# Row clamps and first splits reordered, and float32 operands for one more attention tile, in a fused attention, gated MLP and routed expert kernel

## The chip, the cores and the metric

The kernel runs on one core of a Trainium2 chip. The metric is the device time of one execution in microseconds: the median of three runs. One further execution was recorded by the profiler; durations below come from that one. The engines are TensorE (PE, with PEld for its weight loads), VectorE (DVE), ScalarE (ACT), GpSimd (POOL) and SyncE (SP), which issues most DMAs.

## The reference

What is computed, with the shapes of this case:

```python
# attention: q, k, v (2, 8, 768, 64); n_global 8, n_local 96
scores = q @ k.T / 8 - slope[h] * dist      # local window of 96, and 8 global columns; the rest masked
a = softmax(scores)                          # + 1e-9 in the denominator
x = (a @ v) as (1536, 512)
# gated MLP, d_ff 1536
xn = x / rms(x) * rms_g
x = (silu(xn @ w_gate) * (xn @ w_val)) @ w_out
# routed experts: 8 experts, d_ff 1024, two per token
noisy = x @ w_router + log1p(exp(x @ w_noise)) * noise
top2 = the two largest of noisy; weights = softmax over the two
out[t] = sum over the two experts e of weight * (relu(x[t] @ w1[e]) @ w2[e])
```

The MLP's three weights arrive as 64-bit floats and are brought to float32 in the kernel, from pairs of 32-bit words.

## The kernel before, in words

Everything stays in one program on one core, and the order of each engine's instructions is made by a planner at build time, which plays the program through in its own simulated time and takes the instructions in the order in which they become ready there, earlier lines of the program first. `follow(a, b)` (L262) adds an edge with no wait in it: the planner puts `a` behind `b` in the order. On the chip each engine works through its queue strictly in that order, so an instruction that waits holds up all that is queued behind it.

**Attention.** The 1536 tokens are 12 tiles of 128, six per batch (`NB`). Tile `ti` attends to its own and the preceding tile's keys, and to the first 32 columns. A tile is worked through in four steps of two heads (`scores`, `turn` and `values`, at L358, L388 and L416). Matmuls with full precision are made in two ways. Tiles below `F32T` (L133, value 5: tiles 0 to 4) use float32 operands, one float32 product for the scores and one for the values, which the profile shows as two records each. Tiles from `F32T` on split each operand into a high and a low part: three float32r products for the scores (L372 to L374), and for the values five products of 16-bit parts (L445 to L447). The splits are made on ACT and DVE (L325 to L331, L407, L408) and on POOL (`vsplit`, L300). Tile 5 is the first tile with split operands and the last of batch 0, so `prep` (L306) has a branch (L341 to L350) that splits the keys which it takes over from tile 4, and `values` (L429) splits tile 4's values anew. Tile 6 starts batch 1 and takes nothing over.

**MLP.** `VISITS` lists blocks of two or four tiles by chunks of the 12 slices of d_ff. One step of a block runs `up` for gate and value (matmuls into `pg`, `pv` or one `pz`, L613), `hidden` (L616 and on: `u` on ACT and DVE, `dh` on ACT at L625, `dl`), and `down` (matmuls into `acc`, L639), one step behind. The rest of attention is strewn among the first blocks by `side`. A tile's normalised rows are turned by `norm` (L514): transposes into `px` (L518), `xTh` on ACT (L523), `xTl` on DVE (L524).

**Weights of the MLP.** `conv` (L544) loads one block of words (L553), takes Abs on ACT (L558), clamps (L559, on POOL for later blocks), shifts and combines on DVE (L561, L565, L566), and splits (L568, L569). After attention a pool "b" opens in its place; some of the first blocks loaded then have their words in that pool (`spare`, L547).

**Experts.** `route` scores and ranks tokens for a group of tiles and scatters token number and weight to a table in DRAM by indirect DMAs on POOL (L779). There are units of gathered rows: units 0 and 1 for the first 256 and the remaining rows of the expert that leads early, and units 2 to 8 for the other experts. Unit 0 starts under the last MLP blocks, before the last tiles are routed. For each unit `slots` fetches its table rows (`me`, L820, on SP), clamps the row numbers to the table's end (`ic`, L829, on DVE); `gather` (L838) fetches 128 rows by an indirect DMA on POOL; `turn` transposes them on TensorE (L848) and splits them into `gh` on ACT and `gl` on DVE (L850, L851). `run` (L860 and on) goes through 8 slices: `split` (L592) copies an expert's slab on ACT (L597) and subtracts on POOL or DVE (L599); `up` (L874) gives `zh` and `zl` (L878, L879); `down` (L890 or L896) adds up; the rows are scattered into the output (L932), for later units on top of what stands there (`old`, L856). A slab's load is issued by L804 and L807, the next unit's turns and loads run inside the unit before.

Of the kernel before, what the change touches and what calls it, by code (L numbers as in the profile page):

```python
# [9 lines left out]
F32 = mybir.dt.float32  # L10
# [9 lines left out]
P = 128  # L20
# [85 lines left out]
def fused(ctx: ExitStack, tc: tile.TileContext, q, k, v, n_global, n_local, w_gate, w_val, w_out,  # L106
# [23 lines left out]
    LAG = 8  # L130
    NRAW = {"a": 12, "b": 7}
    NACC = 8
    F32T = 5  # L133
    N2 = 4
    slopes = [2.0 ** (-8.0 * (h + 1) / H) for h in range(H)]

# [125 lines left out]
    def follow(a, b):  # L262
        tc.add_manual_dep(a, b.name, mybir.DependencyInfo(mybir.DependencyClass.NoSync, mybir.DependencyReason.DATA),
                          reason="order")
# [41 lines left out]
    def prep(ti, wide):  # L306
        b, i = divmod(ti, NB)
        t0 = i * P
        nblk = 1 if i == 0 else 2
        W = nblk * P  # L310
        C0 = 2 * P - W
        qn, kn = state.pop(("in", ti))
        full = ti < F32T
        if full:
            kT = [at.tile([P, NP, 2 * P], F32, name=f"kT{ti}", tag="kT0", bufs=2)] * 2
            qT = [at.tile([P, NP, P], F32, name=f"qT{ti}", tag="qT0", bufs=2)] * 2
        else:
            kT = [at.tile([P, NP, 2 * P], F32R, name=f"kT{ti}_{x}", tag=f"kT{x}", bufs=2) for x in range(2)]
            qT = [at.tile([P, NP, P], F32R, name=f"qT{ti}_{x}", tag=f"qT{x}", bufs=2) for x in range(2)]
        for src, dh, dl, sc in ((kn, kT[0][:, :, P:], kT[1][:, :, P:], 1.0), (qn, qT[0], qT[1], -(D ** -0.5))):  # L320
            pt = bank("t", wide, f"pt{ti}")
            p3 = pt.rearrange("p (a b) -> p a b", a=NP)
            for c in range(NP):
                nc.tensor.transpose(p3[:, c, :], src.rearrange("p (a t) d -> p a (t d)", a=NP)[:, c, :], ident)
            nc.scalar.activation(dh, p3, AF.Copy, scale=sc)  # L325
            if full:
                continue
            if sc == 1.0:
                nc.vector.tensor_sub(dl, p3, dh.bitcast(F32))
            else:  # L330
                nc.vector.scalar_tensor_tensor(dl, p3, sc, dh.bitcast(F32), op0=ALU.mult, op1=ALU.subtract)  # L331

        def same(dst, src):
            nc.gpsimd.tensor_scalar(dst, src if src.dtype == F32 else src.bitcast(F32), 1.0, 0.0, op0=ALU.mult, op1=ALU.add)
        parts = 1 if full else 2
        if i == 0:
            kg = [at.tile([P, NP, 32], F32 if full else F32R, name=f"kg{ti}_{x}", tag=f"kg{x}", bufs=1) for x in range(parts)]
            for x in range(parts):
                same(kg[x], kT[x][:, :, P:P + 32])
            state["kg"] = kg  # L340
        elif ti == F32T:  # L341
            ok, pk = state["kg"][0], state["kT"][0][:, :, P + 32:]
            kg = [at.tile([P, NP, 32], F32R, name=f"kg{ti}_{x}", tag=f"kh{x}", bufs=1) for x in range(2)]
            same(kg[0], ok)
            nc.gpsimd.tensor_sub(kg[1], ok, kg[0].bitcast(F32))
            same(kT[0][:, :, 32:P], pk)
            nc.gpsimd.tensor_sub(kT[1][:, :, 32:P], pk, kT[0][:, :, 32:P].bitcast(F32))
            for x in range(2):
                same(kT[x][:, :, :32], kg[x])
            state["kg"] = kg  # L350
        else:
            for x in range(parts):
                same(kT[x][:, :, :32], state["kg"][x])
                same(kT[x][:, :, 32:P], state["kT"][x][:, :, P + 32:])
        state["kT"] = kT
        state["cur", ti] = (W, C0, nblk, kT, qT)
# [59 lines left out]
    def values(u, wide):  # L416
        ti, pr = divmod(u, NP)
        nblk = state["cur", ti][2]
        if pr == 0:
            i = ti % NB  # L420
            if i > 1:
                grows(ti)
            own = [state["own", ti]]
            if i:
                own.insert(0, state["own", ti - 1])
            if ti < F32T:
                state["vs", ti] = [a[0].rearrange("p h d -> p (h d)") for a in own]
            else:
                if ti == F32T:  # L429
                    own[0] = state["own", ti - 1] = vsplit(ti - 1, own[0][0])  # L430
                state["vs", ti] = [(halves(a)[1], halves(b)[1], halves(a)[0]) for a, b in own]
        vs = state["vs", ti]
        ph, pl = state.pop(("pt", u))
        if pr == 0:
            state["po", ti] = bank("o", wide, f"po{ti}")
        po = state["po", ti]
        for t in range(2):
            h = pair[pr][t]
            hs = slice(h * D, (h + 1) * D)
            n = 0  # L440
            if ti < F32T:
                for j in range(nblk):
                    nc.tensor.matmul(po[:, hs], (ph, pl)[t][:, j, :], vs[j][:, hs], start=(j == 0), stop=(j == nblk - 1))
                continue
            for j in range(nblk):  # L445
                for lhs, x in ((ph, 0), (ph, 1), (ph, 2), (pl, 0), (pl, 1)):
                    nc.tensor.matmul(po[:, hs], lhs[:, t, j, :], vs[j][x][:, hs], start=(n == 0),  # L447
                                     stop=(n == 5 * nblk - 1))
                    n += 1
        if pr == NP - 1:  # L450
            rs = sb.tile([P, H], F32, name=f"rs{ti}", tag="rs", bufs=2)
            nc.vector.tensor_scalar(rs, state.pop(("sm", ti)), PSC, PSC * 1e-9, op0=ALU.mult, op1=ALU.add)
            nc.vector.reciprocal(rs, rs)
            x = sb.tile([P, DM], F32, name=f"x{ti}", tag="n2", bufs=N2)
            nc.vector.tensor_mul(x.rearrange("p (h d) -> p h d", h=H), po.rearrange("p (h d) -> p h d", h=H),
                                 rs.rearrange("p (h o) -> p h o", o=1).broadcast_to([P, H, D]))
            state["x", ti] = rms(ti, x)
            del state["cur", ti]
# [55 lines left out]
    def norm(ti, x, wide):  # L514
        pt = bank("t", wide, f"px{ti}")
        p3 = pt.rearrange("p (a b) -> p a b", a=DC)
        for c in range(DC):
            nc.tensor.transpose(p3[:, c, :], x[:, c * P:(c + 1) * P], ident)  # L518
        g, tt = divmod(ti, ST)
        if tt == 0:  # L520
            xTh[g] = sb.tile([P, ST, DC, P], F32R, name=f"xTh{g}", tag="xTh", bufs=3)
            xTl[g] = sb.tile([P, ST, DC, P], F32R, name=f"xTl{g}", tag="xTl", bufs=3)
        nc.scalar.activation(xTh[g][:, tt], p3, AF.Copy)  # L523
        nc.vector.tensor_sub(xTl[g][:, tt], p3, xTh[g][:, tt].bitcast(F32))  # L524


    pools = {"a": sb}
# [16 lines left out]
    def conv(nm, f, src):  # L544
# [14 lines left out]
        (nc.gpsimd if late else nc.vector).tensor_scalar(w, w, HIGH, LOW, op0=ALU.min, op1=ALU.max)  # L559
        wi = w.bitcast(I32)  # L560
        sh = nc.vector.tensor_scalar(wi, wi, 3, 0x3FFFFFF8, op0=ALU.logical_shift_left, op1=ALU.bitwise_and)  # L561
        if f:
            after(ab, "A", min(f, 3) - 1)
            after(sh, "V", min(f, 3) - 1)
# [27 lines left out]
    def split(key, u):  # L592
        pid = "ab" + key[1:]
        src = raw[pid][:, "ab".index(key[0])]
        f = int(key.split("_")[1])
        wp = pools["b"].tile([P, 2, 512], F32R, name=f"s{key}_{u}", tag="ws", bufs=3)
        nc.scalar.activation(wp[:, 0], src, AF.Copy)  # L597
        pool = u == 0 and f < 5 if key[0] == "b" else u >= 2 and f < 3
        (nc.gpsimd if pool else nc.vector).tensor_sub(wp[:, 1], src, wp[:, 0].bitcast(F32))  # L599
        return wp[:, 0], wp[:, 1]  # L600

    x2t = {}

    accs = {}

    def up(f, nm, t0, nt, pz):
# [9 lines left out]
    def hidden(ci, f, t0, nt, pg, pv):  # L616
        GN = nt * P
        hp = pools["b"] if nt > 2 else sb
        u = hp.tile([P, GN], F32, name=f"u{t0}_{f}", tag="u", bufs=1)
        nc.scalar.activation(u, pg, AF.Tanh, scale=0.5)  # L620
        nc.vector.scalar_tensor_tensor(u, u, 1.0, pg, op0=ALU.add, op1=ALU.mult)
        nc.vector.scalar_tensor_tensor(u, u, 0.5, pv, op0=ALU.mult, op1=ALU.mult)
        dh = hp.tile([P, GN], F32R, name=f"dh{t0}_{f}", tag="dh", bufs=2)
        dl = hp.tile([P, GN], F32R, name=f"dl{t0}_{f}", tag="dl", bufs=2)
        nc.scalar.activation(dh, u, AF.Copy)  # L625
        (nc.gpsimd if ci < len(CHUNKS) - 1 else nc.vector).tensor_sub(dl, u, dh.bitcast(F32))  # L626
        return dh, dl

# [180 lines left out]
    class Unit:  # L809
# [13 lines left out]
        def slots(self):  # L823
# [2 lines left out]
                self.fetch()  # L826
            me = self.me
            ic = sb.tile([P, NS], I32, name=f"ic{n}", tag="ic", bufs=3)
            nc.vector.tensor_scalar(ic[:, :ns], me[:, :ns, 0], self.rows - 1, None, op0=ALU.min)  # L829
            self.ic = ic  # L830
            self.gh = sb.tile([P, DC, CAP], F32R, name=f"gh{n}", tag="xTh", bufs=3)
            self.gl = sb.tile([P, DC, CAP], F32R, name=f"gl{n}", tag="xTl", bufs=3)
# [300 lines left out]
```

## Time and profile before

| | us |
|---|---|
| median of three runs | 823.5 (823.29 to 825.07) |
| the profiled execution | 823.71 |
| its span, first to last instruction | 821.9 |
| TensorE busy | 785.8, 96% of the span |
| VectorE, ScalarE, GpSimd busy | 464.1, 358.2, 302.3 |
| mean granted clock of TensorE | 0.990 of full speed |

A row of the profile names the engine, the line, the operation, the tile written and the tiles read, and the count of merged instructions (x4); a bracket at its end gives how long the engine had stood idle just before, and what ended that wait. A float32 matmul shows as two records. Matmuls are pipelined: a record's duration holds the pipeline's length, so the price of a group is the time from its start to the start of the next. "PEclk" is the TensorE clock that was granted in a stretch, as a share of full speed.

### The profile page before, as it was taken

The numbers are of one execution on the slowest core, as the hardware profiler recorded it, in microseconds if no ns is written. First come the engines' busy times: TensorE is split into PE (matmuls) and PEld (weight loads), VectorE is DVE, ScalarE is ACT, GpSimd is POOL, SyncE is SP. The second block draws the span as 40 slices with busy tenths as digits, with TensorE's granted clock in tenths as the row PEclk, the third lists the DMA queues.
The fourth block names the chain that finished last, engine by engine and source line by source line (L and its number), as shares of the span: only waits on it lengthen the run. The fifth ranks groups of instructions, "written<-read, shape, count | busy, mean of one in ns | idle before, by whom it ended". The sixth has DMA issues, their size and how long they took to land. (4 is left out here: it accounts for less than half of the span.)

```text
span 821.9 us, 13918 instructions
## 1 busy us (share of the span) xinstructions
PE 785.8 (96%) x5092; PEld 695.1 (85%) x5097; DVE 464.1 (56%) x1075; ACT 358.2 (44%) x803; POOL 302.3 (37%) x343
## 2 busy tenths in 40 slices
PE   6999999999989999999999997999999999999993
PEld 3678899898978888889998985888999999999982
DVE  4876756666578888424535466544444445445551
ACT  4666656565455344113332463533333434343430
POOL 6354334232068565100423045351424343434311
PEclk9999999999999999999999999999999999999997
DMA  9544313151043330001115303983373729272010
GB/s 198 153 127 117 104 32 73 39 155 53 2 146 112 104 126 26 1 1 52 27 27 137 121 27 98 324 272 120 100 212 121 236 92 279 80 244 74 35 38 34
DMA packets 116808, 88.78 MB, mean 108 GB/s; under 512 B 49417, under 2 KB 100617, under 8 KB 116736
## 3 DMA queue, kind: packets, MB, share of 16 engines
q1 hardware_dynamic: 105136, 65.09, 28.4%
q0 software_dynamic: 7120, 19.27, 7.0%
q10 hardware_dynamic: 4480, 3.49, 1.7%
q8 instruction: 42, 0.69, 0.4%
q14 instruction: 30, 0.25, 0.1%
HBM read 75.18 MB, written 13.34 MB: 108 GB/s over the span
## 5 line engine op out<-in xcount | busy, mean ns | idle before, releaser
L874 PE MATMUL pz<-gh,sa 128*128 128x256 f32 (+7 forms) x576 | 158.1, 340 | 1.8 <-DVE sa L599 0.8
L874 PEld LDWEIGHTS pz<-gh,sa 128*128 128x128 f32 x576 | 104.0, 190 | 8.0 <-DVE sa L599 1.3
L874 PE MATMUL pz<-gl,sa 128*128 128x256 f32 (+7 forms) x288 | 97.6, 339 | 0.9 <-DVE gl L851 0.9
L639 PE MATMUL acc<-wo,dh 128*128 128x512 f32 x288 | 89.7, 404 | 3.6 <-ACT dh L625 3.6
L890 PE MATMUL ac<-zh,sb 128*128 128x480 f32 (+4 forms) x320 | 86.3, 364 | 0.0
L878 ACT ACTIVATE zh<-pz 128x256 fp32r<-128x256 f32 (+7 forms) x72 | 35.1, 487 | 109.9 <-PE pz L874 109.3
L879 DVE SCALAR_TENSOR_TENSOR zl<-pz,zh 128x256 fp32r<-128x256 f32 (+7 forms) x72 | 39.7, 552 | 67.1 <-ACT zh L878 66.9
L597 ACT ACTIVATE sa<-wab 128x512 fp32r<-128x512 f32 x72 | 45.3, 630 | 68.8 <-PE ac L890 40.5
L613 PE MATMUL pz<-xTh,wv 128*128 128x256 f32 x352 | 73.8, 286 | 0.0
L613 PE MATMUL pz<-xTh,wg 128*128 128x256 f32 x352 | 72.6, 285 | 1.0 <-ACT xTh L523 0.7
L639 PEld LDWEIGHTS acc<-wo,dh 128*128 128x128 f32 x288 | 51.2, 189 | 13.9 <-ACT dh L625 4.6
L838 POOL DMA_INDIRECT xg<-x2d,ic x30 | 30.2, 1006 | 88.4 <-PE pg L848 48.3
L613 PEld LDWEIGHTS pz<-xTh,wg 128*128 128x128 f32 x352 | 58.3, 190 | 4.6 <-ACT xTh L523 0.9
L599 DVE TENSOR_TENSOR sa<-wab,sa 128x512 fp32r<-128x512 f32 x51 | 35.3, 693 | 45.4 <-ACT sa L597 45.3
L890 PEld LDWEIGHTS ac<-zh,sb 128*128 128x128 f32 x320 | 57.9, 188 | 3.2
L779 POOL DMA_INDIRECT metad<-meta,si x24 | 24.8, 1033 | 96.4 <-DVE si L758 90.3
L613 PEld LDWEIGHTS pz<-xTh,wv 128*128 128x128 f32 x352 | 57.6, 189 | 0.8 <-issue 0.3
L626 POOL TENSOR_TENSOR dl<-u,dh 128x256 fp32r<-128x256 f32 (+1 forms) x38 | 36.4, 957 | 58.6 <-ACT dh L625 41.0
L383 ACT ACTIVATE p<-s,mx 128x256 f32<-128x256 f32 (+1 forms) x96 | 46.2, 483 | 26.8 <-DVE mx L380 26.8
L874 PEld LDWEIGHTS pz<-gl,sa 128*128 128x128 f32 x288 | 54.6, 190 | 3.8 <-DVE gl L851 1.1
L639 PE MATMUL acc<-wo,dl 128*128 128x512 f32 x144 | 53.4, 401 | 0.0
L599 DVE TENSOR_TENSOR sb<-wab,sb 128x512 fp32r<-128x512 f32 x67 | 48.1, 719 | 8.9 <-ACT sb L597 8.0
(257 smaller groups left out, 1888.9 us busy)
## 6 DMA issues: line engine op xcount, KB each, us to landing
wab<-in_moe_w_dram SPq DMA_DIRECT2D x128, 256.0 KB, 4.9
rg<-in_moe_w_gate_dram SPq DMA_DIRECT2D x12, 512.0 KB, 3.7
rv<-in_moe_w_val_dram SPq DMA_DIRECT2D x12, 512.0 KB, 3.6
ro<-in_moe_w_out_dram SPq DMA_DIRECT2D x12, 512.0 KB, 3.5
kn<-in_k_dram SPq DMA_DIRECT2D x12, 256.0 KB, 3.5
qn<-in_q_dram SPq DMA_DIRECT2D x12, 256.0 KB, 4.1
vn<-in_v_dram SPq DMA_DIRECT2D x12, 256.0 KB, 5.3
out_dram<-zero SPq DMA_DIRECT2D x1, 3072.0 KB, 14.0
```

The source lines that it names most:

```text
L383: nc.scalar.activation(p[:, :W], s[:, :W], AF.Exp, scale=-1.0, bias=mx[:, h:h + 1], accum_out=sm[:, h:h + 1])
L597: nc.scalar.activation(wp[:, 0], src, AF.Copy)
L599: (nc.gpsimd if pool else nc.vector).tensor_sub(wp[:, 1], src, wp[:, 0].bitcast(F32))
L613: nc.tensor.matmul(pz, a[:, cs], x[:, tt:tt + nt, c, :], start=(n == 0), stop=(n == 3 * DC - 1))
L626: (nc.gpsimd if ci < len(CHUNKS) - 1 else nc.vector).tensor_sub(dl, u, dh.bitcast(F32))
L639: nc.tensor.matmul(acc[t], a[:, tt], w, start=(f == CHUNKS[ci][0] and n == 0), stop=(end and n == 2))
L779: st = nc.gpsimd.indirect_dma_start(out=metad, out_offset=bass.IndirectOffsetOnAxis(ap=si[:, t, kk:kk + 1], axis=0), in_=meta[:, G0[g] + t ...
L838: self.last = nc.gpsimd.indirect_dma_start(out=xg[:m], out_offset=None, in_=x2d[:self.rows], in_offset=bass.IndirectOffsetOnAxis(ap=self.i ...
L874: nc.tensor.matmul(pz[:, :cap], a[:, cs], x[:, c, :cap], start=(k == 0), stop=(k == 3 * DC - 1))
L878: nc.scalar.activation(dh[:, :cap], pz[:, :cap], AF.Relu)
L879: nc.vector.scalar_tensor_tensor(dl[:, :cap], pz[:, :cap], 0.0, dh[:, :cap].bitcast(F32), op0=ALU.max, op1=ALU.subtract)
L890: nc.tensor.matmul(acc[c][:, :cap], w[:, c * P:(c + 1) * P], a[:, :cap], start=(f == 0 and k == 0), stop=(f == FB2 - 1 and k == 2))
```

## The change

There are four edits. `F32T` becomes `NB`, 6, so that tile 5 too works with float32 operands; the branches that joined tile 4 to tile 5 go. In `conv`, the Abs and the first shift of the first three blocks with words in pool "b" follow the `xTh` and `xTl` of the tile normalised last. In `split`, the ACT copies of unit 0's slices 0 and 1 follow the fourth-last `dh` of the MLP (`marks[-4]`). The clamp `ic` of all nine units moves from DVE to POOL.

```diff
@@ -130,7 +130,7 @@
-    F32T = 5
+    F32T = NB
@@ -337,16 +337,6 @@
-        elif ti == F32T:
-            ok, pk = state["kg"][0], state["kT"][0][:, :, P + 32:]
-            kg = [at.tile([P, NP, 32], F32R, name=f"kg{ti}_{x}", tag=f"kh{x}", bufs=1) for x in range(2)]
-            same(kg[0], ok)
-            nc.gpsimd.tensor_sub(kg[1], ok, kg[0].bitcast(F32))
-            same(kT[0][:, :, 32:P], pk)
-            nc.gpsimd.tensor_sub(kT[1][:, :, 32:P], pk, kT[0][:, :, 32:P].bitcast(F32))
-            for x in range(2):
-                same(kT[x][:, :, :32], kg[x])
-            state["kg"] = kg
@@ -426,8 +416,6 @@
             else:
-                if ti == F32T:
-                    own[0] = state["own", ti - 1] = vsplit(ti - 1, own[0][0])
                 state["vs", ti] = [(halves(a)[1], halves(b)[1], halves(a)[0]) for a, b in own]
@@ -520,8 +508,9 @@
-        nc.scalar.activation(xTh[g][:, tt], p3, AF.Copy)
-        nc.vector.tensor_sub(xTl[g][:, tt], p3, xTh[g][:, tt].bitcast(F32))
+        hi = nc.scalar.activation(xTh[g][:, tt], p3, AF.Copy)
+        lo = nc.vector.tensor_sub(xTl[g][:, tt], p3, xTh[g][:, tt].bitcast(F32))
+        state["normed"] = hi.ins, lo.ins
@@ -559,6 +548,9 @@
         sh = nc.vector.tensor_scalar(wi, wi, 3, 0x3FFFFFF8, op0=ALU.logical_shift_left, op1=ALU.bitwise_and)
+        if spare and turns["words"] < 6:
+            follow(ab.ins, state["normed"][0])
+            follow(sh.ins, state["normed"][1])
@@ -594,13 +586,15 @@
-        nc.scalar.activation(wp[:, 0], src, AF.Copy)
+        cp = nc.scalar.activation(wp[:, 0], src, AF.Copy)
+        if u == 0 and f < 2:
+            follow(cp.ins, marks[-4])
@@ -622,7 +616,7 @@
-        nc.scalar.activation(dh, u, AF.Copy)
+        marks.append(nc.scalar.activation(dh, u, AF.Copy).ins)
@@ -826,7 +820,7 @@
-            nc.vector.tensor_scalar(ic[:, :ns], me[:, :ns, 0], self.rows - 1, None, op0=ALU.min)
+            nc.gpsimd.tensor_scalar(ic[:, :ns], me[:, :ns, 0], self.rows - 1, None, op0=ALU.min)
```

## Rows read from the trace of the kernel before

**Rows 1.** The page, part 1: busy us, share, instructions.

```profile
PE 785.8 (96%) x5092; PEld 695.1 (85%) x5097; DVE 464.1 (56%) x1075; ACT 358.2 (44%) x803; POOL 302.3 (37%) x343
```

**Rows 2.** Stretches: us; PE, PEld, DVE, ACT, POOL busy (x instructions); PEclk; DMA.

```profile
60.00:220.00 160.00, 160.00 (x1504) 143.85 (x1503) 104.33 (x303) 94.03 (x267) 52.47 (x77) 1.00 0.30 77
...
235.00:428.00 193.00, 192.97 (x1089) 166.05 (x1088) 119.78 (x232) 70.21 (x126) 78.48 (x70) 1.00 0.20 58
```

**Rows 3.** Stretches of L374 (two rows), L447 (one), L443 (three) alone.

```profile
90.08:91.13 1.05, 1.05 (x4) 0.66 (x4) 1.00 0.93 356
...
96.32:97.22 0.90, 0.90 (x6) 0.77 (x6) 1.00 0.93 295
...
222.71:223.31 0.60, 0.60 (x20) 0.60 (x19) 1.00 0.00 0
...
88.70:89.54 0.84, 0.84 (x8) 0.83 (x7) 1.00 1.24 210
...
68.06:68.99 0.93, 0.93 (x8) 0.86 (x8) 1.00 1.18 241
...
64.18:64.54 0.36, 0.36 (x4) 0.36 (x4) 1.00 0.47 119
```

**Rows 4.** ACT, DVE, PE by time: start us, us, what, [idle before].

```profile
231.42 0.66 ACT L558 ACTIVATE wco<-ro 128x512 f32<-128x512 f32 x1 [1.66 <-DMA ro<-in_moe_w_out_dram]
...
231.99 0.40 ACT L625 ACTIVATE dh<-u 128x256 fp32r<-128x256 f32 x1
...
230.25 0.42 DVE L622 SCALAR_TENSOR_TENSOR u<-u,pz 128x256 f32<-128x256 f32 x1
...
231.84 0.75 DVE L505 SCALAR_TENSOR_TENSOR x<-x,ri,grow 128x512 f32<-128x512 f32 x1 [1.16 <-POOL ri L504]
...
232.44 1.19 PE L639 MATMUL acc<-wo,dh 128*128 128x512 f32 x4 [1.79 <-ACT dh L625]
...
233.47 0.60 PE L518 MATMUL px<-ident,x 128*128 128x128 f32 x4
...
234.75 0.50 PE L613 MATMUL pz<-xTh,wg 128*128 128x256 f32 x2 [0.69 <-ACT xTh L523]
```

**Rows 5.** By time, ACT, DVE, POOL, PE; landing of xg, 440 to 460.

```profile
442.56 0.63 ACT L597 ACTIVATE sa<-wab 128x512 fp32r<-128x512 f32 x1 [4.89 <-DMA wab<-in_moe_w_dram]
...
445.69 1.00 DVE L829 TENSOR_SCALAR ic<-me 128x2 int32<-128x2 int32 x1 [0.18 <-DMA me<-metad]
...
448.26 0.95 POOL L838 DMA_INDIRECT xg<-x2d,ic  x1 [0.30 <-issue]
...
443.55 1.82 PE L639 MATMUL acc<-wo,dh 128*128 128x512 f32 x4 [1.85 <-ACT dh L625]
...
456.45 0.63 PE L848 MATMUL pg<-ident,xg 128*128 128x128 f32 x4
...
DMA to landing us min/median/max: 6.2/7.1/8.1
```

**Rows 6.** By time, DVE, PE, POOL; last, a stretch of PE alone.

```profile
510.90 0.17 DVE L829 TENSOR_SCALAR ic<-me 128x4 int32<-128x4 int32 x1 [7.31 <-DMA me<-metad]
...
511.45 0.72 PE L896 MATMUL ac<-sb,zl 128*128 128x512 f32 x2 [4.02 <-DVE zl L879]
...
518.64 0.63 PE L848 MATMUL pg<-ident,xg 128*128 128x128 f32 x4 [0.72 <-DMA xg<-x2d,ic]
...
535.78 0.48 PE L874 MATMUL pz<-gh,sa 128*128 128x480 f32 x1 [0.21 <-POOL sa L599]
...
529.72 0.96 POOL L838 DMA_INDIRECT xg<-x2d,ic  x1 [12.59 <-DVE sa L599]
...
534.43 2.54 POOL L599 TENSOR_TENSOR sa<-wab,sa 128x512 fp32r<-128x512 f32 x2
...
511.40:517.00 5.60, 5.55 (x26) 0.70 0.90 285
```

**Rows 7.** Waits of DVE: us in total, times, longest.

```profile
DVE ic L829 <- DMA me<-metad: 13.7, 7, 7.3
```

## What I expect and why

> **What bounds the kernel now.** I read the page first, then TensorE's busy time by stretches, then its waits, and then, at each wait, the four engines' instructions in order of time. TensorE is busy for 785.8 of 821.9 us [rows 1], and in two long stretches it never stops: 160.00 of 160 us from 60 to 220, 192.97 of 193 us from 235 to 428 [rows 2]. There every matmul that is added is paid in full, and work taken off the other engines is worth nothing. Outside the start and the end TensorE stands still for over 1.5 us at three places only: 1.79 us before 232.44 [rows 4], 1.85 us before 443.55 [rows 5], 4.02 us before 511.45 [rows 6]. Three of the four edits aim at one of these each; the fourth adds matmuls inside the first full stretch. The question at each place is what TensorE waits for next.
>
> **Tile 5 in float32.** Removed: the splits of its keys, queries, probabilities and values, all on ACT, DVE and POOL, where they lie beside a TensorE that is full [rows 2], so they give nothing. Also removed is what joined tile 4 to tile 5; tile 6 opens the second batch with keys of its own and needs no join. On TensorE the scores of two heads take 1.05 us in float32 (4 records) and 0.90 us as three float32r products (6 records); the values of two heads take 0.60 us as twenty 16-bit products, and in float32 0.84, 0.93 or 2 x 0.36 = 0.72 us [rows 3]. Tile 5 has four such pairs: 4 x 0.15 = 0.6 for the scores, 4 x 0.12 to 4 x 0.33 = 0.5 to 1.3 for the values; with the mean of the three float32 rows, 0.83, it is 0.9. Term: **+1.5 us** (1.1 to 1.9), as nothing covers it.
> The Trainium skill (FP8 and Floating Point Precision, TensorE Precision Notes) counts four passes through the array for true FP32. An estimate by passes makes the scores 4/3 of 0.90 and the values 4/5 of 0.60, so that the tile would cost 4 x 0.30 - 4 x 0.12 = +0.7 us. The rows disagree on the values, dearer in float32 and not cheaper.
>
> **The first words of the late pool.** ACT stands 1.66 us on the load of a word (the Abs at 231.42) ahead of the dh that TensorE wants; dh runs at 231.99, though DVE has its input ready at 230.25 + 0.42 = 230.67 [rows 4]. With the Abs of three words behind the last tile's xTh, dh comes 1.32 us earlier. The next thing late is x of tile 11: DVE ends it at 231.84 + 0.75 = 232.59, so its transposes, now at 233.47, start at about 232.65, and all behind them moves by 0.82 us. Term: **-0.8 us**, from 0 (another load ahead on ACT) to -1.3 (the x chain moves too). The three Abs, their clamps on POOL and shifts on DVE come up to 2 us later; their DMA issues stay. These weights serve the next chunk, and in 193 us TensorE waits for no weight [rows 2]; without that cover up to those 2 us would come back.
>
> **The first splits.** The copy of the first expert slab waits 4.89 us for its load ahead of a dh; TensorE runs dry for 1.85 us, and four dh products then take 1.82 us, against 1.19 at 232.44 [rows 4, 5]. Idle and slow clock together are worth some 3.5 us (1.85, and 1.7 as priced below for the third place). But the gathers of unit 0 don't hang on TensorE: their fetch lands at 445.69, where DVE starts the clamp, the second gather goes out at 448.26 and lands 8.1 us later, at 456.36, and TensorE takes up its transposes at 456.45 [rows 5]. It has no slack there. Coming 3.5 us earlier, it stands at the two turns instead. What moves that landing is the clamp: on DVE it took 1.00 us here, 0.17 at 510.90 [rows 5, 6]; on an idle POOL I take 0.3, between these two. Term: **-0.7 us** (0 to -3.5; the last if the planner puts the turns later in TensorE's queue, +2.3 at the other end, below). The up to four moved copies (0.63 us on ACT each [rows 5]) lie among the last steps of the chunk, ahead of unit 0's first matmul; their loads have landed by then, and none of their DMAs moves. On POOL the gathers lose a split that stood ahead of them.
>
> **The row clamps.** Each of nine goes from DVE to POOL, just ahead of the gathers that need it. DVE waits 13.7 us at seven clamps, 7.31 of it at one [rows 6, 7]. In that one the zl behind it waits, and the products behind zl; on POOL only gathers stand behind, which need the clamp anyway. So the 4.02 us go. Then TensorE does its work up to the first turn of unit 2 without a stall, and there needs a gather: even now it waits 0.72 us for it and starts at 518.64 [rows 6]. The gather's chain (scatter, fetch, clamp, gather) doesn't contain the stall. So 518.6 stays, and the idle becomes one piece: 4.02 + 0.72, and 1.7 for the clock, since from 511.40 to 517.00 the granted clock averages 0.70, between its levels of 2.4 and 1.2 GHz, which loses 0.30 x 5.6 us [rows 6]. That loss lies today inside the wait for the gather and is free. After one idle of about 6.4 us the low level of the clock comes behind the gather and is paid: +1.7, less some 0.3 of waits that are still ahead (0.21 before 535.78). Term: **+1.4 us** (-0.7 to +1.9). There is a second cap: at 535.78 TensorE waits for splits that POOL runs only behind the four gathers of the third unit (529.72 to 534.43) [rows 6], so even with later turns no more is to be had than the 0.7 us by which these may start earlier without the hop over DVE, where they wait for the instruction behind the clamp. In the other units POOL waits for the fetch in place of DVE, with old-row gathers, scatters and splits queued behind; DVE's six other waits come to 6.4 us and none shows in TensorE: 0, up to +0.5 where a split stands behind.
> The Trainium skill (TensorE: Matmul & The Clock Gate, HAM oscillation) describes a wait for a DMA after which the array starts again at half speed. The 0.70 behind the 4.02 us agrees with it; it speaks against gathering short idles into a long one.
>
> **Sum.** 1.5 - 0.8 - 0.7 + 1.4 = +1.4 us. The profiled execution took 823.7 us (span 821.9), the median of the runs is 823.5; on the median the forecast is **824.9 us**.
>
> **Rivals.**
> First, the stalls are really gone: the planner, which orders each engine by its own idea of the time, puts the turns of unit 0 some 3 us later in TensorE's queue, so that no gather is waited for. For it: the whole order is remade with each change. Against: a planner that had expected the load so late would not have put the copy ahead of dh; its order already reckons without these stalls, so taking them away need not move the turns in it. 1.5 - 0.8 - 3.5 - 0.7 = -3.5: **820.0 us**.
> The Trainium skill (DMA: Bandwidth & Descriptors, Anatomy of one DMA) gives 2.0 us plus bytes over 436 GB/s, 2.6 us for a gather of 256 KB, as an estimate. By it the gathers would land before TensorE arrives, and this rival would hold. The rows have 6.2 to 8.1 us [rows 5], among weight loads.
> Second, slower: the two waits at unit 0's turns, 1.4 us or more each, bring the low clock there too (+1.7), and the turns stand earlier in the queue, because POOL's gathers have lost the split ahead of them (+1.3, what about a POOL split takes: 2.54 for two [rows 6]). 1.5 - 0.8 + 2.3 + 1.4 = +4.4: **827.9 us**. It decides when an idle loses the clock: 1.79 us did not (four products in 1.19 after it), 1.85 did (1.82).
> Third, the reordering does nothing: another instruction that waits for the same loads stands ahead of dh. 1.5 + 1.4: **826.4 us**.
>
> **How the numbers follow.** 0.2%, 1.65 us, is what a measurement here can tell from no change. Forecast 0.44, first rival 0.29, second 0.21, third 0.06. The forecast lies close under the bound; of its 0.44 I put 0.34 within it and 0.10 above. Faster 0.29, within 0.34, slower 0.10 + 0.21 + 0.06 = 0.37. The range takes both rivals in, and 0.6 more below the first, for tile 5 at 1.1 and a little more near 231: 819.4 to 827.9. The forecast's own is 1.5 either way, 823.4 to 826.4, by the ends of its terms taken together.
>
> **What would show it.** In the trace after: no float32r score in tile 5 and 1.0 to 1.4 us more between its neighbours; dh before the word's Abs near 231, TensorE's idle there 1.6 us in place of 2.5; no wait of ACT for the first slab; no clamp on DVE; and new idle of TensorE before the transposes of gathered rows, in unit 0 (2 to 3 us) and in unit 2 (about 6 us, the granted clock down behind it). If these waits are missing, the first rival was right, and the error is that I kept the order of TensorE's queue. If tile 5 costs nothing, TensorE was not as full as it looks.

## The result, and the profile after

| | before | after |
|---|---|---|
| median of three runs, us | 823.5 | 835.1 (832.1 to 836.5) |
| after over before | | 1.0108 [1.0074, 1.0143] |
| the same kernel in a second set of runs | | 1.0100 [1.0073, 1.0126] |
| the profiled execution, and its span | 823.71, 821.9 | 832.11, 830.4 |
| mean granted clock | 0.990 | 0.986 |

The change costs 1%, 8 to 9 us by the two ratios, where +1.4 was forecast (the two medians of three, taken by themselves, lie 11.6 us apart). The page of after, part 1 (it answers [rows 1]): TensorE has 51 instructions fewer and is busy 3.0 us longer.

```profile
PE 788.8 (95%) x5041; PEld 695.3 (84%) x5041; DVE 459.6 (55%) x1064; ACT 356.5 (43%) x803; POOL 301.1 (36%) x344
```

The waits of TensorE, after: who waited, for whom, us in total, times, longest.

```profile
PE pg L842 <- DMA xg<-x2d,ic: 11.9, 3, 5.4
...
PE lg L719 <- DVE sel L716: 1.2, 1, 1.2
PE pz L607 <- ACT xTh L511: 0.9, 1, 0.9
...
PE acc L633 <- ACT dh L619: 0.5, 1, 0.5
```

The stalls at which three edits aimed are gone: no 1.85 us for dh, no 4.02 us for zl, and of the 1.79 us for the other dh 0.5 are left. In their place stand 11.9 us before transposes of gathered rows, at three turns. Unit 0 first (it answers [rows 5]), then unit 2 (it answers [rows 6]): start, us, what, idle before.

```profile
447.54 0.37 SPq L814 DMA_DIRECT2D me<-metad  x1
449.51 0.24 POOL L823 TENSOR_SCALAR ic<-me 128x2 int32<-128x2 int32 x1 [9.13 <-DMA me<-metad]
450.53 1.22 POOL L832 DMA_INDIRECT xg<-x2d,ic  x1 [0.77 <-POOL ic L823]
452.05 0.96 POOL L832 DMA_INDIRECT xg<-x2d,ic  x1 [0.30 <-issue]
...
451.42 0.39 PE L607 MATMUL pz<-xTh,wv 128*128 128x256 f32 x2
456.95 1.09 PE L842 MATMUL pg<-ident,xg 128*128 128x128 f32 x4 [5.15 <-DMA xg<-x2d,ic]
460.82 1.05 PE L842 MATMUL pg<-ident,xg 128*128 128x128 f32 x4
...
518.13 0.23 POOL L823 TENSOR_SCALAR ic<-me 128x4 int32<-128x4 int32 x1 [5.19 <-DMA me<-metad]
518.84 1.43 POOL L832 DMA_INDIRECT xg<-x2d,ic  x1 [0.47 <-POOL ic L823]
525.90 1.09 PE L842 MATMUL pg<-ident,xg 128*128 128x128 f32 x4 [5.43 <-DMA xg<-x2d,ic]
```

The chain is the one forecast: fetch, clamp (0.24 us on POOL), gather, and 6.4 us later (450.53 to 456.95) the rows. TensorE was there 5.15 us before them. The stretches behind both waits: us; PE, PEld, DVE, ACT, POOL busy; PEclk; DMA share and GB/s.

```profile
451.80:456.95 5.15, 0.00 (x1) 0.03 (x1) 0.00 (x0) 0.00 (x0) 0.96 (x1) 0.80 0.96 297
456.95:462.40 5.45, 5.45 (x22) 4.94 (x23) 2.13 (x4) 1.47 (x3) 0.00 (x0) 0.56 0.86 270
520.47:525.90 5.43, 0.00 (x1) 0.04 (x1) 1.12 (x2) 0.90 (x2) 3.01 (x3) 0.75 1.06 346
525.90:533.13 7.23, 7.23 (x34) 6.41 (x35) 2.98 (x5) 2.77 (x6) 0.00 (x0) 0.71 1.09 332
```

During the waits DVE and ACT have little to do, and behind them TensorE runs 5.45 us at 0.56 and 7.23 us at 0.71: 2.4 and 2.1 us lost.

**Where the 8.5 us lie.** The two profiled executions differ in their first microseconds by chance: the transposes of tile 0 come at 36.84 before and at 34.81 after, in the same order of products; over the profiled executions of kernels that are alike up to there they lie between 34.7 and 37.2. So I lay the marks side by side with the second execution of the changed kernel (`after_again`), which started like that of before. First before, then after:

```profile
36.84 0.61 PE L518 MATMUL px<-ident,x 128*128 128x128 f32 x4
163.50 0.63 PE L518 MATMUL px<-ident,x 128*128 128x128 f32 x4
200.74 0.63 PE L518 MATMUL px<-ident,x 128*128 128x128 f32 x4
499.02 0.63 PE L848 MATMUL pg<-ident,xg 128*128 128x128 f32 x4 [0.36 <-DMA xg<-x2d,ic]
540.28 1.04 PE L848 MATMUL pg<-ident,xg 128*128 128x128 f32 x8
```

```profile
36.96 0.61 PE L506 MATMUL px<-ident,x 128*128 128x128 f32 x4
167.40 0.63 PE L506 MATMUL px<-ident,x 128*128 128x128 f32 x4
237.13 0.63 PE L506 MATMUL px<-ident,x 128*128 128x128 f32 x4
457.32 0.67 PE L842 MATMUL pg<-ident,xg 128*128 128x128 f32 x4 [4.55 <-DMA xg<-x2d,ic]
506.11 0.63 PE L842 MATMUL pg<-ident,xg 128*128 128x128 f32 x4 [1.23 <-DMA xg<-x2d,ic]
525.90 1.09 PE L842 MATMUL pg<-ident,xg 128*128 128x128 f32 x4 [6.71 <-DMA xg<-x2d,ic]
548.80 1.03 PE L842 MATMUL pg<-ident,xg 128*128 128x128 f32 x8
```

| up to | before | after | later by | so this part costs | forecast |
|---|---|---|---|---|---|
| tile 0's transposes | 36.84 | 36.96 | 0.12 | | |
| tile 7's | 163.50 | 167.40 | 3.90 | tile 5: +3.8 | +1.5 |
| tile 11's | 233.47 [rows 4] | 237.13 | 3.66 | first words: -0.2 | -0.8 |
| unit 1's first turn | 499.02 | 506.11 | 7.09 | first splits, clamps of units 0 and 1: +3.4 | -0.7 |
| unit 3's first turns | 540.28 | 548.80 | 8.52 | unit 2's clamp: +1.4 | +1.4 |

Behind that nothing changes: the span ends 8.5 us later. In the first execution the part from tile 11's transposes to unit 1's first turn costs 6.1 us in place of 3.4 (234.85 to 506.46). Of the 2.6 us more, 1.17 are a wait of the route at 410.93 that the second execution doesn't have, 0.6 the longer wait at unit 0's turn, and 0.7 lie behind that turn.

### The profile page after: what moved, and what is told of

Same layout as the page of the kernel before. It is cut to its first block, busy times and chain, and to the rows that moved or that the text cites. A ratio compares the mean times of both kernels' runs of the same rounds, so it can differ in the third digit from the quotient of the medians.

```text
span 830.4 us, 13792 instructions
## 1 busy us (share of the span) xinstructions
PE 788.8 (95%) x5041; PEld 695.3 (84%) x5041; DVE 459.6 (55%) x1064; ACT 356.5 (43%) x803; POOL 301.1 (36%) x344
## 5 line engine op out<-in xcount | busy, mean ns | idle before, releaser
L620 POOL TENSOR_TENSOR dl<-u,dh 128x256 fp32r<-128x256 f32 (+1 forms) x38 | 38.4, 1010 | 58.8 <-ACT dh L619 53.0
L884 PE MATMUL ac<-zl,sb 128*128 128x480 f32 (+4 forms) x160 | 53.0, 357 | 0.0
```

Source lines behind the costliest of these rows:

```text
L884: nc.tensor.matmul(acc[c][:, :cap], w[:, c * P:(c + 1) * P], a[:, :cap], start=(f == 0 and k == 0), stop=(f == FB2 - 1 and k == 2))
```

## The experiments

Times are ratios to runs of the kernel before on the same chip, with 95% intervals; in microseconds they are taken of 823.5. Each run has a label, given with its heading; the text mostly uses its first two characters. A trace is one execution and can differ from the ratio by some microseconds. From the transposes of tile 0 to the end of the span the traces have 5.1 us less for g1 than for the changed kernel, 1.2 more for b1 than for g3 and 3.5 less for b2 than for g3; the ratios below give 7.9, 3.0 and 7.0.

**Each edit alone** (`e1_tile`, `e2_clamp`, `e3_words`, `e4_splits`). Four kernels, each the kernel before with one part of the diff above.

```diff
-    F32T = 5
+    F32T = NB
```

The two branches that joined tile 4 to tile 5 go with it.

> The kernel before with float32 operands for tile 5 and nothing else. By the prices of the rows the tile costs 1.5 us (825.0). The rival: in the trace of the changed kernel the transposes of the rows of tile 7 come 3.7 us later than before, counted from those of tile 0; if all of that belongs to tile 5, this kernel takes 827.2. The places near 231, 443 and 511 us stay as they are but for that shift.

1.0046 [1.0029, 1.0063]: **+3.8 us** (2.4 to 5.2). In its trace the transposes of tile 0 and tile 7 stand at

```profile
35.20 0.61 PE L506 MATMUL px<-ident,x 128*128 128x128 f32 x4
165.68 0.63 PE L506 MATMUL px<-ident,x 128*128 128x128 f32 x4
```

that is 130.48 us apart, against 126.66 before: +3.8 again. Over the eight traces without the edit and with the old order there it is 126.66 to 127.13, over the five with the edit 130.31 to 130.71: 3.6 in the mean. The dear alternative holds, and the price by the rows does not.

```diff
-            nc.vector.tensor_scalar(ic[:, :ns], me[:, :ns, 0], self.rows - 1
+            nc.gpsimd.tensor_scalar(ic[:, :ns], me[:, :ns, 0], self.rows - 1
```

> The kernel before with the nine clamps on POOL and nothing else. If the waits only move to the turns: the 4.0 us before the downs near 511 are gone, TensorE waits 5 to 6 us for the gather at the first turn of unit 2 with the low clock behind it, and unit 0's turns, which now stand 2.3 us earlier in TensorE's queue, wait 1 to 2 us: 825 to 827. If the stall on DVE was a loss of its own: 822.8 or less, and no wait of TensorE for a gather above 1 us.

1.0024 [1.0008, 1.0040]: +2.0 us. The waits moved as expected, to the turns, and POOL's split came late too:

```profile
455.83 0.63 PE L848 MATMUL pg<-ident,xg 128*128 128x128 f32 x4 [1.23 <-DMA xg<-x2d,ic]
...
521.68 0.81 PE L848 MATMUL pg<-ident,xg 128*128 128x128 f32 x4 [3.77 <-DMA xg<-x2d,ic]
...
541.68 0.70 PE L874 MATMUL pz<-gh,sa 128*128 128x480 f32 x2 [1.72 <-POOL sa L599]
```

At unit 1's first turn, too, TensorE waits longer: 1.18 to 1.29 us in the nine traces with the clamp on POOL, 0.35 to 0.40 in the seven with the clamp on DVE. There DVE writes `me` itself just before the clamp, and from that write to the gather it is 0.57 us with the clamp on DVE (494.98 to 495.55 before) and 1.06 with the clamp on POOL (501.49 to 502.55 after). So unit 1's clamp costs 0.9 us, where the prediction had 0 for it.

```diff
+            follow(ab.ins, state["normed"][0])
+            follow(sh.ins, state["normed"][1])
```

> The kernel before with Abs and shift of the first words of the late pool behind the last tile's xTh and xTl, and nothing else. By the rows dh comes 1.3 us and the transposes of tile 11 0.8 us earlier: 822.7. The rival, another load ahead of dh on ACT: 823.5.

1.0010 [0.9995, 1.0025]: not to be told from no change. The interval ends at -0.4 us, so the -0.8 of the first expectation is outside it. The rival's reason fails too, as dh does run ahead of the Abs. In the trace the idle before the downs near 232 falls from 1.79 to 0.52 us, and tile 11's transposes come 0.27 us earlier against tile 10's.

```diff
+        if u == 0 and f < 2:
+            follow(cp.ins, marks[-4])
```

> The kernel before with the first splits of unit 0 behind the fourth-last dh and nothing else. As forecast, the stall goes and TensorE waits 2 to 3 us at unit 0's turns: 822.8. What the changed kernel suggests since: the turns stand 2.3 us earlier in the queue and TensorE comes 3.5 us earlier, so that it waits some 5 us for the gather, with the low clock behind: 825. If the gain is kept: 820.

1.0015 [1.0001, 1.0029]: +1.2 us, no gain. What I had not seen: with the split gone from its place, the clamp, here still on DVE, is next to wait, ahead of the u which dh needs.

```profile
447.33 0.17 DVE L831 TENSOR_SCALAR ic<-me 128x2 int32<-128x2 int32 x1 [5.15 <-DMA me<-metad]
...
448.31 0.42 ACT L627 ACTIVATE dh<-u 128x256 fp32r<-128x256 f32 x1 [4.84 <-DVE u L624]
...
453.37 0.63 PE L850 MATMUL pg<-ident,xg 128*128 128x128 f32 x4 [1.28 <-DMA xg<-x2d,ic]
```

Before, that clamp waited 0.18 us [rows 5], as ACT's wait for the slab had covered the fetch. One stall hid the other.

**The whole change again** (`after_again`). The four sum to +7.8 us.

> The changed kernel once more, to be compared with its variants on one chip. The four edits alone came to +3.8, +2.0, +0.8 and +1.2 us; if they only add up, +7.8; if the edits at unit 0 hinder each other (the turn moves forward once, but the stall that hid the gather is gone at the same time), +9 or more. The waits before the turns of unit 0 and unit 2 near 5 us each are expected again.

1.0100: +8.2 us (6.0 to 10.4). Its waits are those of the rows above. Whether the edits hinder each other can't be told from 7.8 against 8.2.

**Unit 0's turns later** (`g1_turns_later`; without the tile edit, `g3_no_tile_turns_later`). The turns are emitted four and three steps later in the program, each with a `follow` behind the product issued last, in a bank that the route doesn't use.

```diff
-            if kx in (3, 4):
-                units[0].turn(kx - 3)
+            if (ci, t0, f) == (3, 10, 9):
+                units[0].turn(0)
...
+                units[0].turn(1)
...
+                if self.n == 0:
+                    follow(tr.ins, state["pe"])
```

> The changed kernel with unit 0's two turns 5.2 and 7 us later in TensorE's queue. If the 5.15 us that TensorE waits there, and the slow clock behind, are lost because the turns stand too early, it takes 4 to 5.5 us less than the changed kernel, since the last route, and with it unit 2's gathers, come that much earlier. The rival, that the wait only moves on to unit 2's turns: no gain, and a wait of some 10 us there.

1.0004 [0.9984, 1.0023]: 7.9 us less than the changed kernel on the same chip, more than expected (the 5.1 us of the traces are within it). Unit 0's turns wait for nothing now; unit 2's does as before:

```profile
457.59 0.49 PE L844 MATMUL pg<-ident,xg 128*128 128x128 f32 x3
463.62 0.63 PE L844 MATMUL pg<-ident,xg 128*128 128x128 f32 x4
...
519.85 0.45 PE L844 MATMUL pg<-ident,xg 128*128 128x128 f32 x1 [5.86 <-DMA xg<-x2d,ic]
```

The wait did not move on, and so the turn's place in the queue is shown to be what cost it. In the trace unit 1's first turn comes at 499.36 in place of 506.11, 6.8 us earlier; 4.55 of them are the wait and some 1.7 the slow clock behind it.

> As g1_turns_later, and tile 5 as in the kernel before. If float32 in tile 5 costs what it cost alone, 3.8 us less than g1_turns_later, so about the time of the kernel before or up to 1 us less; by the prices of the rows alone, 1.5 less.

The edit is g1's, on the change without its first hunk. 0.9949 [0.9930, 0.9967]: 4.2 us faster than the kernel before, and 4.5 us less than g1. Tile 5's price of about 4 us is confirmed, and the three other edits together with unit 0's moved turns are worth 4 us. The kernel before with nothing but its turns moved was not run; its turns of unit 0 wait for nothing.

**Unit 2's turns later** (`g2_both_later`). As g1, and unit 2's turns stand behind slices 6, 7, 7 and 7 of unit 1, again by `follow`.

```diff
-                if 8 - len(nxt.tiles) <= f:
+                if i == 1:
+                    for s in {6: (0,), 7: (1, 2, 3)}.get(f, ()):
+                        nxt.turn(s)
+                elif 8 - len(nxt.tiles) <= f:
```

> As g1_turns_later, and the four turns of unit 2 some 8 us later in TensorE's queue too. If the 5.4 us wait there is a loss of its own, 4 to 5 us less than g1_turns_later. By the cap that was forecast, unit 2's first matmuls then wait for the splits that POOL runs only behind the gathers of unit 3, and at most 1.5 us comes of it, with a wait for POOL of 3 to 5 us in its place.

1.0035 [1.0016, 1.0053]: 2.6 us more than g1. Unit 2's turn waits for nothing, but two products into unit 2 the first turn of unit 3 does, which the planner has moved forward:

```profile
520.74 0.60 PE L844 MATMUL pg<-ident,xg 128*128 128x128 f32 x4
...
528.90 0.69 PE L872 MATMUL pz<-gh,sa 128*128 128x480 f32 x2 [0.77 <-ACT gh L848]
536.31 1.08 PE L844 MATMUL pg<-ident,xg 128*128 128x128 f32 x4 [6.71 <-DMA xg<-x2d,ic]
```

Its table rows were fetched at 521.75 and landed by 528.77, where POOL's clamp starts. So no more came of it, as the cap had it, but through another door: the gather of the next unit and not POOL's splits.

**The clamps on DVE, turns right** (`b1_dve`). g3 with L829 as in the kernel before.

> As g3_no_tile_turns_later, with the clamps on DVE as in the kernel before. If the wait of DVE for the table rows is a loss of its own, 2 to 4 us more than g3_no_tile_turns_later. If TensorE would wait for the gather of unit 2 anyway, as forecast, the same within 1 us: the downs near 511 wait 3 to 4 us again and the turn behind them little.

0.9986 [0.9967, 1.0005], against 0.9949 for g3: by the ratios 3 us more, with intervals that meet; by the traces 1.2 us more. Of these, 0.8 lie ahead of unit 1's first turn (TensorE waits 1.44 us at 447.01 for a u behind unit 0's clamp, and 0.9 less at unit 1's turn) and 0.35 between the first turns of units 1 and 3. The downs near 510 wait 3.38 us and the turn behind them 1.60, in sum 4.98; g3 waits 3.61 at the turn and 1.00 for POOL's split. At unit 2 the traces fit the second expectation; by the ratios the first is not excluded, so the worth of these clamps stays open.

**All turns right** (`b2_unit2_later`, `b4_later_still`). g3, with unit 2's turns behind slices 5, 6, 7 and 7 of unit 1, unit 3's behind their own slices, and unit 3's table rows fetched with unit 2's.

```diff
-            if self.n != 1:
+            if self.n not in (1, 3):
                 self.fetch()
+            if self.n == 2:
+                units[3].fetch()
```

> As g3_no_tile_turns_later, with unit 2's four turns 5.4 to 6.7 us later and unit 3's turns some 12 us later in TensorE's queue, and the table rows of unit 3 fetched together with those of unit 2. If the wait for a gather is only a matter of where the turn stands, the 3.6 us before unit 2's first turn, the slow clock behind them and the 1.0 us for POOL's split go: 3 to 5 us less. If it moves on to the next unit, as when unit 2's turns alone were put later: no gain or up to 2 us more, with TensorE waiting at unit 3.

0.9864 [0.9839, 0.9889]: **11.2 us faster** than the kernel before, 7 us less than g3, more than expected. A wait of 2.27 us is left at unit 2's first turn, and the clock doesn't fall there.

> As b2_unit2_later, with the first and the third turn of unit 2 behind one slice more. The 2.27 us which TensorE waited there should go, and nothing take their place before unit 2's first product, since turns and splits still end ahead of it: 1 to 2.5 us less than b2_unit2_later. The rival: unit 2's first product then waits for the last splits of its rows, and it is the same time or up to 1 us more.

With unit 2's turns behind slices 6, 6, 7 and 7 (only the first turn moves; the third, which the expectation names too, stood behind slice 7 already): 0.9851 [0.9826, 0.9876], **12.3 us faster** than before, 1.1 us less than b2 but within its interval. The wait falls from 2.27 to 0.89 us:

```profile
455.52 0.55 PE L858 MATMUL pg<-ident,xg 128*128 128x128 f32 x3 [0.92 <-DMA xg<-x2d,ic]
...
519.67 0.52 PE L858 MATMUL pg<-ident,xg 128*128 128x128 f32 x3 [0.89 <-DMA xg<-x2d,ic]
```

How much of the 12.3 us the moved turns and the earlier fetch would bring without the three edits is not shown.

**Float32 or order?** (`h0_tile4`, `b3_tile4`, `o_order`) Between the transposes of tile 0 and tile 7 TensorE makes the same products as before but for tile 5's, and takes 3.8 us longer. Tile 5's own products, but for one score pair of four, lie between the transposes of tile 3 and of tile 6, and there it is 1.9 us, the upper bound of the forecast. Before, then after:

```profile
94.95 0.60 PE L518 MATMUL px<-ident,x 128*128 128x128 f32 x4
144.60 0.60 PE L518 MATMUL px<-ident,x 128*128 128x128 f32 x4
```

```profile
96.41 0.61 PE L506 MATMUL px<-ident,x 128*128 128x128 f32 x4
147.91 0.60 PE L506 MATMUL px<-ident,x 128*128 128x128 f32 x4
```

The other 1.9 us (1.7 by the means of the traces) lie on both sides of it, with the same products and recorded waits that differ by 0.17 us.

```diff
-    F32T = 5
+    F32T = 4
```

> The kernel before, with tile 4 too on split operands (float32 for tiles 0 to 3 only): the tile edit, turned round. By the prices of the products alone 1.5 to 1.7 us less. If float32 in a tile costs 3.8 us as such, 3.8 less. If some 2 us of those 3.8 came from the new order, in which TensorE changes more often from one kind of product to another (13 changes more between the transposes of tile 0 and tile 8, at 0.11 to 0.15 us), it is no gain here: this kernel has 17 changes more than the kernel before, +1.9 to +2.5, so 0 to +1 us.

1.0155 [1.0129, 1.0182]: **+12.8 us**.

> As g3_no_tile_turns_later, with tile 4 too on split operands. As for h0_tile4: 3.8 us less if float32 in a tile costs that as such; no gain if the number of changes between kinds of products decides.

The same edit on g3: 1.0104 [1.0083, 1.0126], 12.8 us more than g3. Both expectations failed, and the test told nothing on its question: in h0 other waits came up (0.62 and 0.39 us near 90, 1.28 and 0.55 us at the downs near 236, 1.43, 0.73 and 0.67 us up to 257, with 1.7 us lost to the clock), and between 510 and 535 the slow clock costs 8.6 us, where before it costs 1.7. The waits up to 257 are nearly all for ACT, DVE and POOL, which make the splits; that these have no time for them near tile 4 is my reading, not shown by a run of its own.

> The kernel before, with the low parts of the values of tiles 4 and 5 made on DVE in place of POOL. TensorE makes exactly the same products, in another order: up to the transposes of tile 9 the same work is done, with 17 changes more from one kind of product to another. If the order of the products is what made 2 of the 3.8 us of the tile edit, the time from the transposes of tile 0 to those of tile 9 grows by 1.5 to 2.5 us without idle of TensorE, and the kernel takes about 2 us more. If the order costs nothing, that time stays within 0.3 us, and the 2 us belong to float32 itself.

```diff
-        nc.gpsimd.tensor_sub(rn, vn, ...
+        (nc.vector if ti < 6 else nc.gpsimd).tensor_sub(rn, vn, ...
```

1.0053 [1.0035, 1.0072]: +4.4 us, with the very same products. Tile 0 and tile 9:

```profile
34.72 0.61 PE L518 MATMUL px<-ident,x 128*128 128x128 f32 x4
200.44 0.63 PE L518 MATMUL px<-ident,x 128*128 128x128 f32 x4
```

165.72 us apart, against 163.90 before: +1.8, of which 0.38 is a recorded wait at 90.46. Over the eight traces with the old order it is 163.90 to 164.37. So an order alone can cost 1.0 to 1.4 us without idle; the rest of the 4.4 lies behind tile 9, where I didn't follow it up, but for two more falls of the clock (3.4 us lost between 233 and 241, 1.7 between 380 and 387). The other 2 of tile 5's 3.8 us may be of this kind. That the number of changes from one kind of product to another is the measure is not shown: 13 changes went with some 2 us in tile 5's case, 17 with 1.0 to 1.4 here, and in h0 the waits hide it.

## Why the prediction was wrong, step by step

**What bounds the kernel: right.** The signs named are there, though not in their size at unit 0: dh ahead of the Abs, no clamp on DVE, no wait of ACT for the first slab, new idle before the gathered rows at both places. Work taken off ACT, DVE and POOL gave nothing, and each stall that was removed showed up at the next thing late.

**Tile 5: the term was mis-sized, +1.5 for +3.8.** The sum of prices was good where tile 5's own products lie (+1.9, its upper end), but it took the order of all others as given. The planner remade it over eight tiles, and some 2 us more went there, in a TensorE that shows no idle for them. That the order is what cost them is likely by o_order, and not shown. "TensorE full" means that no gap is recorded, not that each product runs at its best price. The estimate by passes from the Trainium skill (FP8 and Floating Point Precision, TensorE Precision Notes), +0.7 us, was further off still.

**First words: mechanism right, -0.8 for -0.2.** dh runs ahead of Abs and TensorE's idle falls to 0.5 us. Then x of tile 11 decides, as I had it, but it has become slower itself:

```profile
233.42 0.73 POOL L620 TENSOR_TENSOR dl<-u,dh 128x256 fp32r<-128x256 f32 x1
...
233.49 1.22 DVE L493 SCALAR_TENSOR_TENSOR x<-x,ri,grow 128x512 f32<-128x512 f32 x1 [1.16 <-POOL ri L492]
...
234.85 0.63 PE L506 MATMUL px<-ident,x 128*128 128x128 f32 x4
```

1.22 us against 0.75 [rows 4]: dl on POOL, freed by the same early dh, now runs beside it. That takes back 0.47 us. In all eleven traces in which dl runs beside this x it takes 1.20 to 1.22 us, in the five others 0.75. The Trainium skill (GPSIMD Engine Reference, Specifications) says that GpSimd's way to SBUF is shared with VectorE and that DVE instructions with two SBUF inputs contend for it; x has two, and the trace agrees.

**First splits and unit 0: the step that failed, -0.7 for +3.4.** I forecast 2 to 3 us of new idle before unit 0's turns, and no slow clock behind it; it is 4.55 us in the second execution and 5.15 in the first, with the slow clock. Three things in the step were off. The turn stands 2.3 us earlier in TensorE's queue (eight pz of one product group, two of the next and five downs no longer precede it). I had this only in the slower rival, at 1.3, for its very reason: POOL's gathers lost the split ahead of them. Nor do the gathers come earlier: counted from the u's near 428 (2.9 us later after), the first goes out 0.7 us later and not earlier (0.25 in the second execution), since the scatters took 8.1 us to the fetch in place of 7.4, and from the clamp's start to the gather's it still takes 1.0 us on POOL, where it took 1.3 with the clamp on DVE. And the term was made for both edits together; e4 shows that alone the split only hands its wait to the clamp. With the measured sizes of the second execution the step comes out: 4.55 us of idle, 1.7 of slow clock and 0.9 at unit 1's turn are new, 1.85 of idle and 1.7 of slow clock are gone, +3.6 in sum beside the +3.4 of the table.

**Row clamps, unit 2: right, +1.4 for +1.4.** I forecast one idle of about 6.4 us with the clock's loss behind it; it is 6.71 us in the second execution and 5.43 in the first. The chain doesn't contain the stall, so TensorE waits for the same gather: counted from unit 1's first turn, unit 2's starts 19.62 us later before and 19.79 after. What I had at 0 is the clamp of unit 1, which costs 0.9 us. What the clamps on POOL are worth where unit 0's turns stand right stays open, between 1.2 us (the traces of b1 and g3) and 3.0 (the ratios).

**Rivals.** The second one, slower, is what happened: a wait at unit 0's turns (at the first alone, not at both), the turns earlier in the queue, the slow clock. With the two sizes measured since, 2.3 for 1.3 and 3.8 for 1.5, its 827.9 becomes 831.2, beside 832.1 in the profiled execution and 835.1 in the median. So of what the range was short at its upper end 2.3 us are tile 5, whose bounds I had taken from prices alone, and 1.0 the turn's place; the 3.9 us from there to the median of three I can't account for. The first rival needed the planner to put the turns later; it put them earlier, and g1 to b4 show that the rival's gain was there to be had. The estimate of 2.6 us for a gather, by the Trainium skill (DMA: Bandwidth & Descriptors, Anatomy of one DMA), would have spoken for it; the gather took 6.4 us.

## What to carry to other kernels

Before removing a stall, find the transfer for which that engine waits next and where its consumer stands in the queue: if the transfer's chain doesn't contain the stall, move the consumer by as much as the stall was long, in the same change (here, without the tile edit and with unit 3's fetch earlier, a gain of 1.5%). The planner put such consumers 4.5 to 6.7 us ahead of their rows, and in g2 did so again at the next unit; that it reckons with transfers that are too short is my reading, as its own times are not on record. And where a planner orders everything, price an edit in a full stretch by the whole stretch, not by its own products.

## What the runs showed of the hardware

The granted clock also fell where TensorE had not stopped at all. In e4_splits (us; PE busy; PEclk; DMA share and GB/s):

```profile
370.00:379.80 9.80, 9.80 (x80) 1.00 0.30 109
379.80:383.40 3.60, 3.60 (x19) 0.53 0.00 0
383.40:400.00 16.60, 16.60 (x132) 1.00 0.12 33
```

TensorE is busy for all of 9.80 us ahead of it; between 376.3 and 378.9 it made the router's products of 16 columns each. The same happened there, between 380 and 387, in three more of the 16 profiled executions (b2, b4, o_order), at a loss of 1.7 us each time, and not in the others; it is part of why single executions of one kernel differ by some microseconds. At the waits for gathers, and counted over them too, 1.7, 3.4 or 5.1 us were lost (both executions of the changed kernel, g2). The Trainium skill (TensorE: Matmul & The Clock Gate, HAM oscillation) tells of a wait for a DMA after which the array starts at half speed; with the waits the traces agree (0.56 behind 5.15 us), but the fall in e4_splits has no wait ahead of it. Nor did the length of an idle alone decide: behind 2.42 us of it (e1, at 447.96) the clock stayed at 1.00, behind 1.85 us (before, at 443.55) it was 0.69 up to 449.00.
